# Top-k attention and two MLPs on one core: seven token chunks of 256 and 384 in place of six of 384

## The chip, the cores and the metric

The kernel runs on one core of a Trainium2 chip, in one launch. The metric is the device time of that core in microseconds (us), the median of several runs. Engines are named as the profile names them: PE (TensorE, with PEld for its weight loads), DVE (VectorE), ACT (ScalarE), POOL (GpSimd) and SP (SyncE, which issues every DMA here).

## The reference

```
# attention: batch 4, heads 8, sequence 576, head size 64, float32
scores = q @ k.T / 8
kth    = the 32nd largest score of each row
scores = where(scores >= kth, scores, -1e9)
attn   = exp(scores - max) / (sum + 1e-9)
a      = attn @ v                        # then [2304 tokens, 512]

# first MLP, w_in [512, 2048], w_out [2048, 512]
h = a @ w_in ;  y = (h - tanh(h)) @ w_out

# second MLP, same sizes
h = y @ w_in ;  out = where(h > 0, h, exp(min(h, 0)) - 1) @ w_out
```

## The kernel before

The 2304 tokens are cut into chunks (`CHUNKS`, L35). A chunk is a list of pieces (batch, first token, length). For each chunk and each of the four pairs of heads, attention is done in units: one unit per head where a piece has 256 tokens or more, and one unit for both heads together where it is shorter. A unit is made of tiles of 128 queries, and units are packed into groups of at most three tiles. In all there are 144 tiles, each of 128 queries by 576 keys.

The top-k of a tile is found on DVE: four times the eight largest values (`vm`, MAX8, L318) with three replacements of these by a very small number in between (`w`, MATCH_REPLACE8, L332). The 32nd value is then the threshold. The mask is applied in one of two ways: on DVE, which multiplies the exponentials that ACT has made by (score >= threshold) (L339), or on ACT, by a steep Prelu and an Exp (L334, L335). `MASK_ACT` says for how many tiles of a group in each chunk ACT does it.

The MLP of a chunk has 2 x 16 steps, one for each MLP and each block of 128 hidden columns. A step makes h from the chunk's tokens by 12 matmuls as wide as the chunk (`first`, L460: float32 is carried as a high and a low part, three products, four blocks of the contraction each), then the gate (`gate`: tanh or exp on ACT, `g` on DVE or by `GATE_GP` on POOL, the high part `gh` on ACT, the low part `gl` on POOL), and adds it to the output by three 512-wide matmuls for each 128 tokens (`second`, L496). The first two steps of the second MLP (`PARTED`) make h in two parts by columns.

The first time that weights are used they are prepared (`prepare`, L149 to L169): the raw 512 KB half is loaded, ACT, POOL, DVE (`wf`, L167) and ACT and POOL again turn it into a high and a low part, and the result is kept for the first chunk and written to DRAM. There are 64 such halves. Later chunks load them back (`wt`, L183), 1 MB for each step of each chunk, whatever the chunk's length.

The order is written out in ticks, four for a group: attention of chunk i+1 is laid beside the MLP steps of chunk i, with a group's loads, splits, scores, top-k and transposes at fixed distances. `starts` gives the tick of a chunk's first MLP step, and the MLP of the last chunk has nothing beside it. On top of this a scheduler orders each engine's instructions when the program is built, so the order that stands on an engine is seen in the built program and not in the source. Engines wait for each other by semaphores, and each works through its own list in order.

Of the kernel before, what the change touches and what calls it, by code (L numbers as in the profile page):

```python
# [8 lines left out]
F32 = mybir.dt.float32  # L9
F32R = mybir.dt.float32r  # L10
# [9 lines left out]
P = 128  # L20
# [12 lines left out]


CHUNKS = [  # L35
    [(0, 0, 384)],
    [(0, 384, 192), (1, 0, 192)],
    [(1, 192, 384)],
    [(2, 0, 384)],
    [(2, 384, 192), (3, 0, 192)],  # L40
    [(3, 192, 384)],
]
SIZES = [sum(n for _, _, n in c) for c in CHUNKS]
NMAX = max(SIZES)

MASK_ACT = [3, 1, 0, 0, 0, 0]

GATE_GP = [0, 0, 1, 1, 1, 2]

# [6 lines left out]

WI_BUFS = 5
WO_BUFS = 6  # L60
RAW_BUFS = 3
G_BUFS = 3
T_BUFS = 3
QR_BUFS = 2
KR_BUFS = 2
QS_BUFS = 2
KK_BUFS = 3
# [3 lines left out]
Y_BUFS = 3  # L71
E_BUFS = 6
W_BUFS = 3
G_BUFS = 3
T_BUFS = 3

FIRST_TICK = -8


SPARE = [5, 5, 5, 5, 5, 5]  # L80

QUICK = 6


NU = 384
# [1 line left out]
WHOLE = 1  # L87


DONE = [4, 8, 8, 8, 8, 8]  # L90


@with_exitstack
def tile_topk_attention_two_mlps(
# [11 lines left out]
    def pool(name, bufs, space=None):  # L106
        kw = {} if space is None else {"space": space}
        return ctx.enter_context(tc.tile_pool(name=name, bufs=bufs, **kw))

    const = pool("const", 1)  # L110
    sb = pool("sb", 2)
# [13 lines left out]
    def split(hi, lo, src):  # L125
        nc.scalar.activation(hi, src, copy)  # L126
        nc.gpsimd.tensor_sub(lo, src, f(hi))  # L127

    def bank(tag, name, bufs):
        return ps.tile([P, 512], F32, tag=tag, name=name, bufs=bufs)  # L130
# [15 lines left out]
    def prepare(m, ft, half):  # L146
# [3 lines left out]

        raw = sb.tile([P, 512], I64, tag="wr", name=f"wr{m}_{ft}_{half}", bufs=RAW_BUFS)
        nc.sync.dma_start(raw, (w1, w2)[m][ft][:, half * 512 : half * 512 + 512])
# [41 lines left out]
    for ci, size in enumerate(SIZES):  # L194
        for p in range(NPAIR):
# [22 lines left out]
            for us in cuts:  # L218
                g = Group()
# [11 lines left out]
    def hurried(u):  # L231

        return u.rush and u.last

    def quick(u):

        return u.ci < QUICK and u.p == NPAIR - 1 and u.g.at == chunk_end[u.ci] - 1

    def load_q(u):
        u.qraw = sb.tile([P, NU], F32, tag="qraw", name=f"qraw{u.id}", bufs=QR_BUFS)  # L240
        src = qT[u.b, 2 * u.p + u.heads[0] : 2 * u.p + u.heads[-1] + 1, :, u.q0 : u.q0 + u.n].rearrange("h d s -> d h s")
        nq = u.n * len(u.heads)
        for half in range(1 if u.whole else 2):
            nc.sync.dma_start(u.qraw[half * D : half * D + D, :nq].rearrange("d (h s) -> d h s", s=u.n), src)
# [54 lines left out]
    def topk_steps(g, r):  # L299
# [10 lines left out]

        by_act = 0 if g.rush and hurried(g.units[-1]) else min(k, MASK_ACT[g.units[0].ci])
        if r == 3 and by_act:
# [136 lines left out]
    def first(ci, m, ft):  # L449
        n = SIZES[ci]  # L450
        xh, xl = x_tiles[ci] if m == 0 else z_tiles[ci]
        h = bank("h", f"h{ci}_{m}_{ft}", 2)[:, :n]
        wv = weights.pop((ci, m, ft, 0)).rearrange("p a (k c) -> p a k c", c=P)
        jobs = [(wi, xs, kt) for wi, xs in ((0, xh), (1, xh), (0, xl)) for kt in range(4)]
        if m == 0 and ft == 0:
            jobs.sort(key=lambda x: x[2])
        late = (n // P - 1) * P
        for cs in (slice(0, late), slice(late, n)) if m == 1 and ft < PARTED and late else (slice(0, n),):
            for a, (wi, xs, kt) in enumerate(jobs):
                nc.tensor.matmul(h[:, cs], wv[:, wi, kt], xs[:, kt, cs], start=(a == 0), stop=(a == len(jobs) - 1))  # L460
        t = sb.tile([P, NMAX], F32, tag="t", name=f"t{ci}_{m}_{ft}", bufs=T_BUFS)[:, :n]
        if m == 0:
            nc.scalar.activation(t, h, AF.Tanh)
        else:
            nc.scalar.activation(t, h, AF.Relu, scale=-1.0)  # L465
            nc.scalar.activation(t, t, AF.Exp, scale=-1.0)  # L466
        parts[ci, m, ft] = h, t

    def gate(ci, m, ft):
        n = SIZES[ci]  # L470
        h, t = parts[ci, m, ft]
        g = sb.tile([P, NMAX], F32, tag="g", name=f"g{ci}_{m}_{ft}", bufs=T_BUFS)[:, :n]
        if m == 1:
            nc.vector.scalar_tensor_tensor(g, t, -1.0, h, op0=ALU.add, op1=ALU.max)  # L474
        elif ft % 4 < GATE_GP[ci]:
            nc.scalar.activation(g, h, copy)
            nc.gpsimd.tensor_sub(g, g, t)
        else:
            nc.vector.tensor_sub(g, h, t)  # L479
        gh = sb.tile([P, NMAX], F32R, tag="gh", name=f"gh{ci}_{m}_{ft}", bufs=G_BUFS)[:, :n]  # L480
        gl = sb.tile([P, NMAX], F32R, tag="gl", name=f"gl{ci}_{m}_{ft}", bufs=G_BUFS)[:, :n]
        split(gh, gl, g)
        parts[ci, m, ft] = gh, gl

# [49 lines left out]
    def step_parts(i):  # L534

        ci, m, ft = steps[i]
        nxt = steps[i + 1] if i + 1 < len(steps) else None
        turn = m == 0 and ft == NF - 1
        early = nxt is not None and not turn

        def a():
            if early:
                first(*nxt)

        def b():
            if early:
                gate(*nxt)

        def c():
            second(ci, m, ft)  # L550
            if turn:
                between(ci)
                first(*nxt)
                gate(*nxt)
            if m == 1 and ft == NF - 1:
                store(ci)
            load_next()

        return a, b, c
# [26 lines left out]

    n_ticks = 4 * len(groups) + DONE[-1]
    starts = [4 * e + d for e, d in zip(chunk_end, DONE)]
    at_tick = {}
    for ci in range(len(SIZES) - 1):  # L590
        ticks = starts[ci + 1] - starts[ci] - SPARE[ci]
        for j in range(ticks):
# [3 lines left out]
    for tick in range(FIRST_TICK, n_ticks):  # L596
# [8 lines left out]
        if tick == starts[0]:  # L605
            first(*steps[0])
            gate(*steps[0])
# [71 lines left out]
```

## Time and profile before

| | |
|---|---|
| time, median of 3 runs | 1267.47 us (1267.06 to 1269.64) |
| the profiled execution: its time, its span | 1266.36 us, 1264.3 us |
| PE busy | 1175.6 us, 93% |
| DVE busy | 992.0 us, 78% |
| ACT busy | 785.0 us, 62% |
| POOL busy | 603.2 us, 48% |
| moved by DMA | 286 MB, mean 226 GB/s |

The span is cut below at the first tanh of each chunk's MLP (171.8, 385.5, 565.0, 755.0, 940.9 and 1121.0 us). Called stages: stage A lasts to the first of them and has the attention of the first chunk, with a little of the second; stage 0 has the MLP of chunk 0 beside the attention of chunk 1 and the rest of the weight preparation; stages 1 to 4 have the MLP of that chunk beside the attention of the next; the last stage has the MLP of the last chunk alone. A matmul's duration in the trace is longer than the distance to the next one, since matmuls overlap; what a run of them costs is read from the starts.

### The profile page before, as it was taken

Reading aid. Unit: us, or ns where it says so; the run is one execution under the profiler, and the core shown is the slowest. Engines: PE = TensorE matmul, PEld = TensorE weight load, DVE = VectorE, ACT = ScalarE, POOL = GpSimd, SP = SyncE. Lnnn points to the kernel's source line nnn. Section 1 sums busy time; section 2 is a strip of 40 time slices with the busy share of each in tenths; the row PEclk is TensorE's granted clock in tenths of the full one; section 3 lists DMA queues with packets and bytes.
Section 4 is the critical chain, followed back from the end, with each engine's and each line's share of the span. In section 5 each row is a group of like instructions: output and inputs, shape, how many; then the busy total and the mean of one; then the engine's idle time right before and its main releaser. Section 6 shows DMA issues by size and latency. Waiting matters only on the chain.

```text
span 1264.3 us, 19733 instructions
## 1 busy us (share of the span) xinstructions
PE 1175.6 (93%) x6424; PEld 976.2 (77%) x6424; DVE 992.0 (78%) x1951; ACT 785.0 (62%) x1716; POOL 603.2 (48%) x629
## 2 busy tenths in 40 slices
PE   4477889989999999999999999999999999999998
PEld 2233467878779888888878888888888978889897
DVE  7999999999999999689999579898789988100111
ACT  5898868778876566465646566666555655433333
POOL 4786459779983433243433334434333422233222
PEclk9976699999999999999999999999999999999999
DMA  7886347988779665667657677756666546667672
GB/s 246 312 292 235 90 143 251 314 282 262 241 255 353 222 220 197 208 227 258 218 167 229 208 234 253 234 187 232 209 232 239 198 164 209 199 230 263 216 242 85
DMA packets 97446, 286.12 MB, mean 226 GB/s; under 512 B 12096, under 2 KB 27968, under 8 KB 97344
## 3 DMA queue, kind: packets, MB, share of 16 engines
q1 hardware_dynamic: 97344, 284.87, 67.4%
q8 instruction: 51, 0.84, 0.3%
q14 instruction: 51, 0.42, 0.1%
HBM read 246.55 MB, written 38.27 MB: 225 GB/s over the span
## 4 chain that ended last, share of the span: by engine, by line
PE 69%; DVE 14%; ACT 8%; DMA 5%; issue 3%; POOL 1%; SPq 0%; ACTq 0%; DVEq 0%; POOLq 0%
PE h L460 27%; PE acc L496 27%; PE av L378 6%; DVE vm L318 5%; DVE w L332 4%; DMA wr<-in_w_dram 4%; PE pt L360 4%; DVE wf L167 2%; PE ps L295 2%; PE ps L296 2%; DVE e L339 1%; ACT s L297 1%; ACT wr L162 1%; POOL wr L164 1%; ACT e L334 1%
## 5 line engine op out<-in xcount | busy, mean ns | idle before, releaser
L127 POOL TENSOR_TENSOR gl<-g,gh 128x384 fp32r<-128x384 f32 x192 | 206.1, 1075 | 315.0 <-ACT gh L126 292.1
L318 DVE MAX8 vm<-w 128x8 f32<-128x576 f32 x432 | 319.2, 751 | 3.9
L496 PE MATMUL acc<-wt,gh 128*128 128x512 f32 x1008 | 271.1, 398 | 0.7 <-ACT gh L126 0.7
L332 DVE MATCH_REPLACE8 w<-vm,w 128x576 f32<-128x576 f32 x288 | 213.3, 741 | 0.0
L496 PEld LDWEIGHTS acc<-wt,gh 128*128 128x128 f32 x1008 | 184.1, 188 | 33.9 <-ACT gh L126 1.6
L360 PE MATMUL pt<-ident,e 128*128 128x128 f32 (+1 forms) x720 | 119.7, 295 | 50.7 <-ACT e L335 35.8
L297 ACT ACTIVATE s<-ps 128x288 f32<-128x288 f32 (+1 forms) x320 | 124.5, 406 | 64.0 <-PE ps L296 56.5
L318 DVE MAX8 vm<-s 128x8 f32<-128x576 f32 x144 | 108.2, 752 | 62.0 <-ACT s L297 61.4
L360 PEld LDWEIGHTS pt<-ident,e 128*128 128x128 f32 (+1 forms) x720 | 90.1, 143 | 78.2 <-ACT e L335 42.0
L496 PE MATMUL acc<-wt,gl 128*128 128x512 f32 x504 | 149.9, 399 | 0.3 <-POOL gl L127 0.2
L460 PE MATMUL h<-zh,wt 128*128 128x384 f32 (+2 forms) x768 | 147.6, 325 | 2.6 <-ACT zh L515 1.8
L126 ACT ACTIVATE gh<-g 128x384 fp32r<-128x384 f32 x192 | 100.7, 526 | 74.7 <-DVE g L474 42.5
L460 PE MATMUL h<-xh,wt 128*128 128x384 f32 x672 | 144.7, 340 | 0.5 <-DVE g L479 0.2
L474 DVE SCALAR_TENSOR_TENSOR g<-t,h 128x384 f32<-128x384 f32 x96 | 52.3, 544 | 111.5 <-ACT t L466 111.3
L361 ACT ACTIVATE ph<-pt 128x384 f32<-128x384 f32 (+1 forms) x240 | 109.2, 491 | 40.9 <-PE pt L360 39.9
L460 PEld LDWEIGHTS h<-zh,wt 128*128 128x128 f32 x768 | 123.5, 188 | 13.5 <-ACT zh L515 3.2
L460 PEld LDWEIGHTS h<-xh,wt 128*128 128x128 f32 x672 | 117.7, 188 | 9.1 <-issue 1.2
L339 DVE SCALAR_TENSOR_TENSOR e<-s,vm,e 128x576 f32<-128x576 f32 x115 | 116.8, 1022 | 1.6 <-ACT e L322 0.5
L496 PEld LDWEIGHTS acc<-wt,gl 128*128 128x128 f32 x504 | 92.1, 188 | 20.2 <-issue 2.1
L164 POOL TENSOR_TENSOR wr<-wr,tiny 128x512 f16<-128x512 f32 x64 | 90.5, 1420 | 35.5 <-ACT wr L162 28.8
L332 DVE MATCH_REPLACE8 w<-vm,s 128x576 f32<-128x576 f32 x144 | 106.8, 741 | 0.0
L465 ACT ACTIVATE t<-h 128x384 f32<-128x384 f32 x96 | 46.9, 488 | 95.7 <-PE h L460 95.0
(80 smaller groups left out, 2018.2 us busy)
## 6 DMA issues: line engine op xcount, KB each, us to landing
wt<-w SPq DMA_DIRECT2D x336, 512.0 KB, 4.2
wr<-in_w_dram SPq DMA_DIRECT2D x64, 512.0 KB, 5.4
w<-wp SPq DMA_DIRECT2D x64, 512.0 KB, 4.2
kraw<-in_kT_dram SPq DMA_DIRECT2D x120, 144.0 KB, 3.9
vraw<-in_vL_dram SPq DMA_DIRECT2D x64, 160.0 KB, 3.1
qraw<-in_qT_dram SPq DMA_DIRECT2D x88, 96.0 KB, 3.3
out_dram<-o SPq DMA_DIRECT2D x16, 256.0 KB, 4.9
out_dram<-o SPq DMA_DIRECT2D x4, 128.0 KB, 4.7
```

The costliest lines, as they stand in the source:

```text
L126: nc.scalar.activation(hi, src, copy)
L127: nc.gpsimd.tensor_sub(lo, src, f(hi))
L164: nc.gpsimd.tensor_mul(top, scaled, tiny)
L297: nc.scalar.activation(s[lo:hi, cs], pt[lo:hi, :HS], copy)
L318: nc.vector.max(g.vm[:, j, min(r, 1)], u.s[t] if r == 0 else g.w[j])
L332: nc.vector.match_replace(g.w[j], v, u.s[t] if r == 0 else g.w[j], FILL)
L339: nc.vector.scalar_tensor_tensor(u.e[t], u.s[t], v[:, 7:8], u.e[t], op0=ALU.is_ge, op1=ALU.mult, accum_out=g.sum[:, j : j + 1])
L360: nc.tensor.transpose(pt[:kn, j * P : j * P + P], v.e[t][:, k0 : k0 + kn], ident)
L361: nc.scalar.activation(g.ph[:kn, blk, :nq], pt[:kn, :nq], copy)
L378: nc.tensor.matmul(pt[h * D : h * D + D, :n], v.vraw[h][:kn, blk], v.g.ph[:kn, blk, cs], start=(blk == 0), stop=(blk == NB - 1),)
L460: nc.tensor.matmul(h[:, cs], wv[:, wi, kt], xs[:, kt, cs], start=(a == 0), stop=(a == len(jobs) - 1))
L496: nc.tensor.matmul(acc[ci, m][t], gx[:, t * P : t * P + P], wt[:, wi], start=(ft == 0 and k == 0), stop=(ft == NF - 1 and k == 2),)
```

## The change

The tokens are cut into seven chunks of 256, 384, 384, 384, 384, 256 and 256. Four chunks are whole pieces of one batch, the fifth and sixth are made of two pieces, the last of one. `MASK_ACT` is 3 for the first two chunks: all tiles of the second chunk are masked on ACT, where one of three was before. `GATE_GP` and the other lists by chunk get a seventh entry; the sixth chunk keeps 2 and the seventh has 2. There are six buffers for raw weight halves instead of three, and three for q instead of two. The tiles t, g, gh and gl have the pool's two buffers each instead of three.

```
 CHUNKS = [
-    [(0, 0, 384)],
-    [(0, 384, 192), (1, 0, 192)],
-    [(1, 192, 384)],
+    [(0, 0, 256)],
+    [(1, 0, 384)],
     [(2, 0, 384)],
-    [(2, 384, 192), (3, 0, 192)],
-    [(3, 192, 384)],
+    [(3, 0, 384)],
+    [(1, 384, 192), (2, 384, 192)],
+    [(3, 384, 192), (0, 256, 64)],
+    [(0, 320, 256)],
 ]
-MASK_ACT = [3, 1, 0, 0, 0, 0]
+MASK_ACT = [3, 3, 0, 0, 0, 0, 0]
-GATE_GP = [0, 0, 1, 1, 1, 2]
+GATE_GP = [0, 0, 1, 1, 1, 2, 2]
-RAW_BUFS = 3
-G_BUFS = 3
-T_BUFS = 3
-QR_BUFS = 2
+RAW_BUFS = 6
+QR_BUFS = 3
-SPARE = [5, 5, 5, 5, 5, 5]
-QUICK = 6
+SPARE = [5, 5, 5, 5, 5, 5, 5]
+QUICK = 7
-DONE = [4, 8, 8, 8, 8, 8]
+DONE = [4, 8, 8, 8, 8, 8, 8]
...
-        t = sb.tile([P, NMAX], F32, tag="t", name=f"t{ci}_{m}_{ft}", bufs=T_BUFS)[:, :n]
+        t = sb.tile([P, NMAX], F32, tag="t", name=f"t{ci}_{m}_{ft}")[:, :n]
...
-        gl = sb.tile([P, NMAX], F32R, tag="gl", name=f"gl{ci}_{m}_{ft}", bufs=G_BUFS)[:, :n]
+        gl = sb.tile([P, NMAX], F32R, tag="gl", name=f"gl{ci}_{m}_{ft}")[:, :n]
```

Counted in the built programs, the work on each engine between the first MLP steps of the chunks is this (DVE: MAX8, MATCH_REPLACE8, masks, weight steps `wf`, gates; PE: matmuls of the MLP's first and second part; the stages of after carry their chunk's number).

| stage | before: MAX8, replace, mask, wf, gate | after | before: PE h, acc | after |
|---|---|---|---|---|
| A | 112, 83, 5, 29, 0 | 78, 58, 2, 29, 0 | 0, 0 | 0, 0 |
| 0 | 102, 78, 19, 35, 32 | 105, 80, 5, 35, 32 | 408, 276 | 408, 180 |
| 1 to 4 | 362, 271, 91, 0, 116 | 349, 261, 87, 0, 116 | 1632, 1155 | 1632, 1155 |
| 5 | 0, 0, 0, 0, 24 | 44, 33, 12, 0, 24 | 408, 297 | 408, 189 |
| 6 | | 0, 0, 0, 0, 24 | | 408, 204 |

On PE, where the first chunk's MLP begins, its name in the rows being h0_0_0 (chunk, MLP, block), this stood before; the transposes ahead of it belong to the third tile of the first chunk's last group:

```order
L360 MATMUL pt0_3_0_3_0_0_1_3_1315<-ident_66,e0_3_0_0_1_2_1151 128x128
L360 MATMUL pt0_3_0_3_0_0_1_4_1320<-ident_66,e0_3_0_0_1_2_1151 64x128
L460 MATMUL h0_0_0_1518<-xh0_499,wp0_0_0_1196 128x384 x2
L460 MATMUL h0_0_0_1518<-xl0_500,wp0_0_0_1196 128x384
L460 MATMUL h0_0_0_1518<-xh0_499,wp0_0_0_1196 128x384 x2
```

In the changed kernel, this stands there:

```order
L357 MATMUL pt0_3_0_3_0_0_0_4_989<-ident_66,e0_3_0_0_0_1_833 64x128
L292 MATMUL ps1_0_1_0_0_2_0_0_1021<-kk1_0_1_0_0_0_886,qs1_0_1_0_0_883 128x288
L293 MATMUL ps1_0_1_0_0_2_0_0_1021<-kk1_0_1_0_0_0_886,qs1_0_1_0_0_883 128x288
L457 MATMUL h0_0_0_1291<-xh0_427,wp0_0_0_1001 128x256 x2
L457 MATMUL h0_0_0_1291<-xl0_428,wp0_0_0_1001 128x256
L457 MATMUL h0_0_0_1291<-xh0_427,wp0_0_0_1001 128x256 x2
```

Eight tiles of attention fewer stand ahead of the first step, which is 256 columns wide; lines after the constants are three less than before.

On DVE, in the middle of stage 0, the end of a group of the second chunk (e1 is its second chunk's mask, g0 the gate of the first chunk's MLP) stood before as:

```order
L339 SCALAR_TENSOR_TENSOR e1_1_1_0_0_1_2290,sum1_1_1_1_1_0_0_2219<-s1_1_1_0_0_1_1989,vm1_1_1_1_1_0_0_2217,e1_1_1_0_0_1_2290 128x576
L318 MAX vm1_1_1_1_1_0_0_2217<-w31_1_1_1_1_0_0_2_2222 128x8
L479 TENSOR_TENSOR g0_0_11_2389<-h0_0_11_2361,t0_0_11_2374 128x384
L332 MATCH_REPLACE w31_2_1_2_0_384_0_0_2481<-vm1_2_1_2_0_384_0_2478,w31_2_1_2_0_384_0_0_2481 128x576
L339 SCALAR_TENSOR_TENSOR e1_1_1_0_0_2_2291,sum1_1_1_1_1_0_0_2219<-s1_1_1_0_0_2_2074,vm1_1_1_1_1_0_0_2217,e1_1_1_0_0_2_2291 128x576
```

The masks of the same pair of heads now stand on ACT:

```order
L331 ACTIVATE e1_1_1_0_0_2_1708<-s1_1_1_0_0_2_1497,nk1_1_1_1_1_0_0_1837 128x576
L294 ACTIVATE s1_1_1_0_1_2_1802<-ps1_1_1_0_1_2_0_1_1803 128x288
L294 ACTIVATE s1_1_1_0_1_2_1802<-ps1_1_1_0_1_2_1_1_1807 128x288
L257 ACTIVATE qs1_2_1_0_1_2095<-qraw1_2_1_0_1_1913 128x384
L123 ACTIVATE kk1_3_1_0_0_0_2349<-kraw1_3_1_0_0_0_2149 128x576
L460 ACTIVATE t0_0_11_2060<-h0_0_11_2047 128x256
L332 ACTIVATE e1_1_1_0_0_0_1706,sum1_1_1_1_1_0_0_1621<-e1_1_1_0_0_0_1706,b21_1_1_1_1_0_0_1838 128x576
L123 ACTIVATE gh0_0_10_2021<-g0_0_10_2019 128x256
```

DVE's mask instructions of that chunk left its list, and two ACT instructions for each stand between the copies of scores and gates.

## Rows read from the trace of the kernel before

**Rows 1.** The page's first lines: busy time, share, instructions.

```profile
span 1264.3 us, 19733 instructions
PE 1175.6 (93%) x6424; PEld 976.2 (77%) x6424; DVE 992.0 (78%) x1951; ACT 785.0 (62%) x1716; POOL 603.2 (48%) x629
```

**Rows 2.** Windows, one per stage: stretch, length, each engine's busy us (instructions), clock, DMA.

```profile
0.00:172.00 172.00, 113.01 (x369) 64.53 (x369) 157.45 (x317) 137.87 (x299) 105.55 (x122) 0.82 0.67 221
172.00:385.50 213.50, 195.38 (x1163) 164.26 (x1164) 210.04 (x375) 171.47 (x366) 184.58 (x171) 0.99 0.80 266
385.50:565.00 179.50, 178.05 (x1011) 153.47 (x1010) 159.82 (x330) 105.21 (x239) 65.01 (x72) 1.00 0.70 232
565.00:755.00 190.00, 188.57 (x1048) 159.44 (x1047) 161.28 (x327) 112.69 (x253) 72.08 (x79) 1.00 0.65 217
755.00:941.00 186.00, 184.32 (x1152) 161.57 (x1151) 160.84 (x321) 112.69 (x252) 78.54 (x82) 1.00 0.69 226
941.00:1121.00 180.00, 178.84 (x986) 150.38 (x985) 127.34 (x259) 95.50 (x215) 56.81 (x65) 1.00 0.59 200
1121.00:1264.00 143.00, 137.45 (x705) 122.52 (x703) 15.23 (x27) 49.60 (x100) 40.59 (x40) 1.00 0.61 211
```

**Rows 3.** Groups by line, DVE in stage A: count | busy, mean ns | idle before.

```profile
L318 DVE MAX8 vm<-w 128x8 f32<-128x576 f32 x81 | 59.6, 748 | 0.0
L332 DVE MATCH_REPLACE8 w<-vm,w 128x576 f32<-128x576 f32 x54 | 40.0, 742 | 0.0
...
L167 DVE SCALAR_TENSOR_TENSOR wf<-sc,wr 128x512 uint32<-128x512 uint32 x22 | 14.9, 678 | 2.5 <-POOL wr L164 2.4
L167 DVE SCALAR_TENSOR_TENSOR wf<-wr 128x512 uint32<-128x512 uint32 x7 | 6.1, 875 | 0.0
...
L339 DVE SCALAR_TENSOR_TENSOR e<-s,vm,e 128x576 f32<-128x576 f32 x4 | 4.0, 993 | 0.0
```

**Rows 4.** The same for DVE in stage 0.

```profile
L318 DVE MAX8 vm<-w 128x8 f32<-128x576 f32 x79 | 58.2, 746 | 0.4
L167 DVE SCALAR_TENSOR_TENSOR wf<-wr 128x512 uint32<-128x512 uint32 x35 | 42.7, 1221 | 0.3 <-POOL qs L261 0.3
L332 DVE MATCH_REPLACE8 w<-vm,w 128x576 f32<-128x576 f32 x52 | 38.3, 738 | 0.0
L339 DVE SCALAR_TENSOR_TENSOR e<-s,vm,e 128x576 f32<-128x576 f32 x21 | 26.7, 1277 | 0.0
...
L474 DVE SCALAR_TENSOR_TENSOR g<-t,h 128x384 f32<-128x384 f32 x16 | 8.6, 539 | 0.6 <-ACT t L466 0.5
```

**Rows 5.** The same for ACT in stage 0.

```profile
L335 ACT ACTIVATE e<-e,b 128x576 f32<-128x576 f32 x7 | 5.4, 777 | 0.0
L334 ACT ACTIVATE e<-s,nk 128x576 f32<-128x576 f32 x7 | 5.4, 773 | 0.2 <-POOL nk L324 0.2
```

**Rows 6.** Timeline of PE in the last stage: start, us, instructions merged.

```profile
1154.21 1.56 PE L496 MATMUL acc<-wt,gh 128*128 128x512 f32 x6
...
1156.31 1.55 PE L460 MATMUL h<-xh,wt 128*128 128x384 f32 x8
1157.69 0.86 PE L460 MATMUL h<-xl,wt 128*128 128x384 f32 x4
...
1192.00 0.63 PE L460 MATMUL h<-zl,wt 128*128 128x256 f32 x4
...
1192.47 1.00 PE L460 MATMUL h<-zh,wt 128*128 128x128 f32 x8
...
1193.31 1.13 PE L460 MATMUL h<-zl,wt 128*128 128x256 f32 x8
```

**Rows 7.** The chain that ended last: start, us, what; two attention products.

```profile
462.18 3.52 PE av L378 x20
...
788.97 3.70 PE av L378 x40
```

**Rows 8.** Windows: the busiest 30 us of the DMA engines; columns as in Rows 2.

```profile
380.00:410.00 30.00, 30.00 (x171) 27.65 (x170) 29.46 (x65) 19.89 (x46) 11.04 (x14) 1.00 1.03 354
```

More of the change, by code (lines that the diff above doesn't have):

```diff
@@ L73 @@
 W_BUFS = 3
-G_BUFS = 3
-T_BUFS = 3
 FIRST_TICK = -8
-SPARE = [5, 5, 5, 5, 5, 5]
-QUICK = 6
+SPARE = [5, 5, 5, 5, 5, 5, 5]
+QUICK = 7
 NU = 384
 WHOLE = 1
-DONE = [4, 8, 8, 8, 8, 8]
+DONE = [4, 8, 8, 8, 8, 8, 8]
 @with_exitstack
@@ L471, in gate @@
         h, t = parts[ci, m, ft]
-        g = sb.tile([P, NMAX], F32, tag="g", name=f"g{ci}_{m}_{ft}", bufs=T_BUFS)[:, :n]
+        g = sb.tile([P, NMAX], F32, tag="g", name=f"g{ci}_{m}_{ft}")[:, :n]
         if m == 1:
@@ L479, in gate @@
             nc.vector.tensor_sub(g, h, t)
-        gh = sb.tile([P, NMAX], F32R, tag="gh", name=f"gh{ci}_{m}_{ft}", bufs=G_BUFS)[:, :n]
-        gl = sb.tile([P, NMAX], F32R, tag="gl", name=f"gl{ci}_{m}_{ft}", bufs=G_BUFS)[:, :n]
+        gh = sb.tile([P, NMAX], F32R, tag="gh", name=f"gh{ci}_{m}_{ft}")[:, :n]
+        gl = sb.tile([P, NMAX], F32R, tag="gl", name=f"gl{ci}_{m}_{ft}")[:, :n]
         split(gh, gl, g)
```

## The prediction

> **What bounds the kernel now.** I read the page's first lines, then cut the span into stages by the first tanh of each chunk, then looked in each stage at which engine never rests, and at last at the cost of one instruction of that engine. PE is busy 93% of the span and DVE 78% [rows 1], but no engine is the bound throughout. The reader is to see in the stages [rows 2] that DVE binds the first two, with 157.45 of 172.0 us and 210.04 of 213.5, while PE works little in the first (113 us by its records, at a mean granted clock of 0.82) and in the second waits for what DVE hands over. From 385.5 us on PE is busy to within 1.2 to 1.7 us in each of the four middle stages and 5.5 us in the last, and it is the bound to the end. So a gain in DVE's work counts in stages A and 0, a change of PE's work counts after them, and anything else is hidden.
>
> **The change part by part.**
>
> *Stage A.* By the count of the built programs DVE does 34 MAX8, 25 replacements and 3 masks fewer before the first MLP step: 34 x 0.748 + 25 x 0.742 + 3 x 0.993 = 47.0 us [rows 3]. Records on DVE overlap a little: the groups of this stage add up to 175.7 us over all lines where 157.45 were busy [rows 2], so the time is 0.896 of that, 42.1 us. The 29 weight steps stay. DVE's idle time of 14.55 us stays too, except 2.5 us in which it waited for POOL's pass over a raw half [rows 3]; three more raw buffers let that pass run ahead. Stage A: 172.0 - 42.1 - 2.5 = 127.4 us.
>
> *Stage 0.* DVE gets 3 MAX8 and 2 replacements more, 3.7 us; 14 masks fewer at 1.277, 17.9 us; and 32 gates 256 wide. For these I take 0.41 us, between two thirds of the present 0.539 (0.36) and all of it, so 4.1 us less [rows 4]. Together -18.3 us, times 0.909 (210.04 busy where the groups add up to 231.0): -16.6 us, so 196.9 us. PE's work in this stage, by the prices worked out below, falls from 185.5 to 135.6 us, so PE is not the bound there. Nor is its clock: the granted clock, a mixture of 1.2 and 2.4 GHz, was 0.82 of the upper level over stage A and 0.99 over stage 0 [rows 2], and even 0.82 throughout would make 136 into 166 us, which fits into 197.
>
> *The masks on ACT.* Each costs two passes, 0.773 + 0.777 us [rows 5], and 14 exponentials of about the same 0.775 leave. With 17 more masks that is +26 and -11 us, and the narrower gates, wider whole pieces and fewer splits of k take about 15 us back, so ACT stays near its 171 us of work, now in 197 us: 0.87 busy against 0.80. I count nothing for it, because DVE at 0.98 still hides it; if ACT could be no busier than it is now, stage 0 would be 214 us, 17 us more.
>
> *A rule on the two engines that share a door.* In stage 0 the mask takes 1.277 us on DVE against 0.993 in stage A, and `wf` with both inputs in SBUF 1.221 against 0.678 for the form with one input in PSUM [rows 3, 4]; POOL is busy 0.86 of stage 0 and 0.61 of stage A [rows 2], while MAX8 with one input keeps 0.746 and 0.748. The Trainium skill, page "SBUF — State Buffer", section "Who interferes with whom", says that a VectorE instruction with two SBUF inputs and a GpSimd instruction that reads SBUF exclude each other, the later waiting for the whole of the earlier, and that one with a single SBUF input is not touched. The trace agrees. By that rule the masks that leave also free POOL, but the same 64 raw halves now pass through POOL in 324 us and not 385, so the 35 `wf` of stage 0 would stay near 1.2 us; the sum by it is the same within 2 us, but a large relief is spoken against.
>
> *Stages 1 to 4.* On PE I price by the distance of starts [rows 6]: nine 512-wide products in 2.10 us, 0.233 each; eight 384-wide in 1.38, 0.1725 each; four 256-wide in 0.47, 0.118 each; eight 128-wide in 0.84, 0.105 each. Scores, 288 wide, I take at 0.129, by width. An attention product of a head pair costs 3.52 us in ten 384-wide matmuls and 3.70 in twenty 192-wide [rows 7]; 256 wide I take 2.35 by width, and the 64-wide at the 192-wide price, 0.188 each, as the upper end. With the counts of the built program, the four stages of before are 709.6 us of PE and took 735.5 (a factor of 1.036, for switches between kinds of matmul and short waits); after they are 709.2 by the same prices, so they take 735.1. MLP work is unchanged there, whole pieces save a few scores and the 64-wide pieces give it back.
>
> *Stages 5 and 6 for the last stage.* Before: 138.0 us of PE (408 h products at 67.5, 297 acc at 69.3, transposes 1.3), and it took 143.3; the 5.3 us are the turn between the MLPs and the last store. After, stage 5 is 47.5 for h, 44.1 for acc, and 25.7 for the attention of the last chunk with its transposes: 117.3, times 1.036 is 121.6 us. Stage 6 is 96.0 and again 5.3: 101.3 us. A narrower product costs no more than its width, 0.118 against two thirds of 0.1725, 0.115: weight loads do not show at 256 columns. Together 222.9 us in place of 143.3, +79.6.
>
> *Buffers of t, g, gh and gl.* Two instead of three cost nothing in my sum: h has two banks before and after, so a gate two steps on must wait for the first in either kernel. Below, nothing is to be gained; above, as much as PE idles in the present last stage (5.5 us [rows 2]) once more in each of the last two, 11 us.
>
> *Loads.* A step loads 1 MB of weights whatever its width, so a seventh chunk adds 33.6 MB, and in stage 6 a step of 12 x 0.118 + 6 x 0.233 = 2.8 us wants 374 GB/s. The busiest 30 us gave 354 GB/s [rows 8]. Eleven weight tiles, 5.8 MB, are loaded ahead; stages 5 and 6 together want 2 x 33.6 MB and, for the last attention and the output, some 7 MB, so 74 MB in 223 us, 332 GB/s. I count nothing, since this lies under 354.
>
> *Sum.* Stage A -44.6, stage 0 -16.6, stages 1 to 4 -0.4, the end +79.6: +18.0 us. The span goes from 1264.3 to 1282.3; the profiled execution's time lies 2.1 us over its span and the median 1.1 us over that, so 1285.5. Since three of the prices are upper ends (64-wide products, all DVE idle time but 2.5 us, the full factor in stage 5), I take 3.5 us off: 1282 us. What the shorter end gains (42 us) and the shorter start (61 us) is more than taken back by the stage that is added between (122 us), because PE's work is the same for every token and DVE still has 24 tiles and 35 weight steps in the stage where the MLP has become short.
>
> **The rivals.**
>
> *DVE's stretch goes away (faster).* With six raw buffers, ACT and POOL prepare ahead, and DVE meets POOL less. If `wf` fell to the undisturbed 0.678 in stage 0, that is 35 x 0.543 x 0.909 = 17.3 us, and if of the 18.0 us that DVE idles in the two stages only the start's 7 us stayed, 8.5 more than I counted: 1282 - 26 = 1256 us. It decides from a `wf` below about 0.85 us together with half of that idle time. For it: 0.875 was seen in stage A [rows 3]. Against it: POOL becomes busier, not idler, in the shorter stages.
>
> *DMA binds the last two stages (slower still).* 74 MB at the 300 GB/s that a mixed stretch may give take 247 us and not 223: 1306 us. It decides below 332 GB/s. For it: the mean of stage 0, with many kinds of loads, was 266 GB/s at a share of 0.80, which is 333 at a full share [rows 2]. Against it: 354 in the busiest stretch, and buffers filled in stage 4, which moves only some 200.
>
> *ACT binds stage 0 (slower still).* As priced above: 1299 us.
>
> *The terms cancel.* If half of the first rival comes true, or the factor of 1.036 does not hold, 1267 us within 3.
>
> **How the numbers follow.** Forecast 0.50 (its own range 1272 to 1293), DMA 0.13, ACT 0.05, DVE's relief 0.22, cancelled 0.10. The range of 8 in 10 runs from 1256 to the DMA rival's 1306. 0.2% is 2.5 us, about what can be told from no change. Slower by more has the forecast, DMA and ACT, 0.68; the same 0.10; faster 0.22.
>
> **What would show it.** In the profile after: the first tanh near 127 us and that of the second chunk near 324; DVE busy over 0.95 of stage 0 and PE idle or waiting there, with records well under the 91% of now; `wf` from raw halves still near 1.2 us; the 256-wide products 0.118 us apart; stages 5 and 6 near 122 and 101 us. I am wrong if the second chunk's MLP begins before 306 us, or if the four stages after it take less than 715 us. More than 235 us for the last two stages, with DMA share near 1, would be the DMA rival.

## The result and the profile after

The changed kernel takes 1275.4 us, median of 4 runs (1274.3 to 1276.6), against 1268.4 us for the kernel before in 4 runs. The ratio is 1.0059 (95% interval 1.0041 to 1.0076): slower by some 7 us. The forecast was 1282 us and slower, so the way is right and the size is about half of what was forecast. The profiled execution has a span of 1273.5 us, 9.2 more than before. Two executions, one of the kernel before and the profiled one of e4 below, ran at a granted clock of 0.67 and 0.66 and took 1974.5 and 1671.3 us; they are left out of all times here.

Cut at the first tanh of each chunk, as in [rows 2], the windows of the changed kernel are these: stage A, stage 0, stages 1 to 4 in one row, stage 5 and stage 6. Columns as there.

```profile
0.00:128.70 128.70, 84.81 (x284) 46.44 (x284) 116.76 (x228) 112.20 (x257) 103.93 (x121) 0.99 0.88 305
128.70:317.40 188.70, 155.73 (x910) 127.34 (x911) 183.42 (x348) 161.92 (x381) 155.53 (x164) 0.92 0.81 281
317.40:1050.20 732.80, 725.36 (x4286) 625.27 (x4285) 586.54 (x1188) 429.25 (x973) 294.84 (x318) 1.00 0.71 227
1050.20:1174.60 124.40, 123.31 (x825) 105.57 (x824) 82.96 (x173) 72.12 (x196) 45.45 (x67) 1.00 0.81 279
1174.60:1273.50 98.90, 93.99 (x602) 83.88 (x600) 11.43 (x26) 37.42 (x96) 29.48 (x40) 0.99 0.82 310
```

In us, with DVE's busy time in brackets (the end is the last stage before, stages 5 and 6 after):

| stage | before | forecast | after |
|---|---|---|---|
| A | 172.0 (157.5 DVE) | 127.4 | 128.7 (116.8 DVE) |
| 0 | 213.5 (210.0 DVE) | 196.9 | 188.7 (183.4 DVE) |
| 1 to 4 | 735.5 | 735.1 | 732.8 |
| the end | 143.3 | 121.6 + 101.3 | 124.4 + 98.9 |

The start (stages A and 0) is 68 us shorter and the end 80 us longer. DVE is the busiest engine of the first two stages as before, PE of all later ones. In stage 0 the groups that answer to [rows 4] are these, in the same columns:

```profile
L315 DVE MAX8 vm<-w 128x8 f32<-128x576 f32 x81 | 59.5, 747 | 0.4
L329 DVE MATCH_REPLACE8 w<-vm,w 128x576 f32<-128x576 f32 x53 | 39.1, 738 | 0.0
L164 DVE SCALAR_TENSOR_TENSOR wf<-wr 128x512 uint32<-128x512 uint32 x35 | 38.1, 1090 | 1.3 <-POOL wp L124 1.1
...
L471 DVE SCALAR_TENSOR_TENSOR g<-t,h 128x256 f32<-128x256 f32 x16 | 6.3, 404 | 0.1
L336 DVE SCALAR_TENSOR_TENSOR e<-s,vm,e 128x576 f32<-128x576 f32 x4 | 4.2, 1061 | 0.0
```

The 256-wide gate came at 0.404 us (0.41 was taken), `wf` at 1.090 (near 1.2 was expected). DVE works 183.4 of the stage's 188.7 us and PE 155.7, which is what the prediction named as the sign that DVE binds. On PE, the timeline of stage 6 answers to [rows 6] (start, us, instructions):

```profile
1201.13 1.09 PE L493 MATMUL acc<-wt,gh 128*128 128x512 f32 x4
1202.06 0.63 PE L493 MATMUL acc<-wt,gl 128*128 128x512 f32 x2
1202.53 1.10 PE L457 MATMUL h<-xh,wt 128*128 128x256 f32 x8
1203.47 0.63 PE L457 MATMUL h<-xl,wt 128*128 128x256 f32 x4
1203.94 1.10 PE L493 MATMUL acc<-wt,gh 128*128 128x512 f32 x4
```

Twelve 256-wide products take 1.41 us (0.1175 each) and six 512-wide 1.40 (0.233), so a step is 2.81 us, as priced. Loads kept up with these steps, at 310 GB/s over the stage and a DMA share of 0.82.

### The profile page after: what moved, and what is told of

It is laid out like the page before. It is cut to its first block, busy times and chain, and to the rows that moved or that the text cites. A ratio compares the mean times of both kernels' runs of the same rounds, so it can differ in the third digit from the quotient of the medians.

```text
span 1273.5 us, 21441 instructions
## 1 busy us (share of the span) xinstructions
PE 1183.2 (93%) x6900; PEld 988.5 (78%) x6900; DVE 981.1 (77%) x1961; ACT 812.9 (64%) x1898; POOL 629.2 (49%) x709
## 4 chain that ended last, share of the span: by engine, by line
PE 74%; ACT 12%; DVE 7%; DMA 3%; issue 2%; POOL 1%; SPq 0%; ACTq 0%; POOLq 0%; DVEq 0%
PE h L457 30%; PE acc L493 29%; PE av L375 6%; PE pt L357 4%; DVE vm L315 3%; DMA wr<-in_w_dram 3%; DVE w L329 2%; PE ps L292 2%; PE ps L293 2%; ACT e L332 1%; ACT wr L159 1%; ACT wp L123 1%; ACT ph L358 1%; ACT s L294 1%; DVE wf L164 1%
## 5 line engine op out<-in xcount | busy, mean ns | idle before, releaser
L124 POOL TENSOR_TENSOR gl<-g,gh 128x384 fp32r<-128x384 f32 (+1 forms) x224 | 206.7, 925 | 347.9 <-ACT gh L123 309.2
L493 PE MATMUL acc<-wt,gh 128*128 128x512 f32 x1056 | 290.9, 400 | 1.2 <-ACT gh L123 1.2
L457 PE MATMUL h<-zh,wt 128*128 128x384 f32 (+2 forms) x912 | 162.4, 313 | 2.7 <-ACT zh L512 2.0
L123 ACT ACTIVATE gh<-g 128x384 fp32r<-128x384 f32 (+1 forms) x224 | 107.2, 482 | 77.9 <-DVE g L471 37.7
L457 PE MATMUL h<-xh,wt 128*128 128x384 f32 (+1 forms) x800 | 156.1, 319 | 0.5 <-DVE g L476 0.2
L358 ACT ACTIVATE ph<-pt 128x384 f32<-128x384 f32 (+2 forms) x280 | 116.5, 450 | 43.0 <-PE pt L357 41.9
L471 DVE SCALAR_TENSOR_TENSOR g<-t,h 128x384 f32<-128x384 f32 (+1 forms) x112 | 54.3, 487 | 97.6 <-ACT t L463 95.0
L462 ACT ACTIVATE t<-h 128x384 f32<-128x384 f32 (+1 forms) x112 | 49.6, 444 | 91.9 <-PE h L457 91.3
L124 POOL TENSOR_TENSOR kk<-kraw,kk 128x576 fp32r<-128x576 f32 x64 | 93.5, 1461 | 29.3 <-ACT kk L123 21.7
L375 PE MATMUL av<-ph,vraw 128*64 128x384 f32 (+7 forms) x720 | 103.5, 409 | 0.0
```

Source lines behind the costliest of these rows:

```text
L358: nc.scalar.activation(g.ph[:kn, blk, :nq], pt[:kn, :nq], copy)
L375: nc.tensor.matmul(pt[h * D : h * D + D, :n], v.vraw[h][:kn, blk], v.g.ph[:kn, blk, cs], start=(blk == 0), stop=(blk == NB - 1),)
L493: nc.tensor.matmul(acc[ci, m][t], gx[:, t * P : t * P + P], wt[:, wi], start=(ft == 0 and k == 0), stop=(ft == NF - 1 and k == 2),)
```

## The experiments

Each kernel was timed beside the kernel before, and ratios are to that; lengths come from its profiled execution, cut in the same way. That one execution lies up to 4 us from the median (e8's is 3.8 us under it, e2's 2.6 over), so a difference of a few us between two lengths is near the noise. The table holds what all of them say together, in us. "Start" is stages A and 0, with DVE's busy time in them; "rest" is all that comes after. "Masks" are the masks of the second chunk on ACT, "raw" is the number of buffers for raw weight halves, and "six whole" is the chunking of e3.

| kernel | median us | ratio (interval) | start: DVE busy of length | rest |
|---|---|---|---|---|
| before | 1266.5 to 1268.4 | 1 | 367.5 of 385.5 | 878.8 |
| changed | 1275.4 | 1.0059 (1.0041 to 1.0076) | 300.2 of 317.4 | 956.1 |
| e1, before + masks | 1273.9 | 1.0058 (1.0041 to 1.0075) | 346.0 of 393.4 | 879.1 |
| e2, changed - masks | 1280.7 | 1.0112 (1.0097 to 1.0126) | 309.2 of 321.9 | 959.6 |
| e3, six whole + masks | 1269.9 | 1.0025 (1.0017 to 1.0034) | 344.1 of 378.8 | 888.3 |
| e7, two chunks of 256 first | 1291.0 | 1.0190 (1.0176 to 1.0204) | 269.0 of 303.6 | 983.3 |
| e5, changed, 3 raw | 1292.0 | 1.0203 (1.0188 to 1.0219) | 310.3 of 333.5 | 956.5 |
| e8, before, 5 raw | 1275.0 | 1.0060 (1.0046 to 1.0074) | 367.0 of 391.8 | 877.6 |
| e9, before, 5 raw + masks | 1280.0 | 1.0103 (1.0089 to 1.0117) | 350.9 of 400.1 | 877.8 |
| e10, six whole, 5 raw | 1283.2 | 1.0129 (1.0114 to 1.0143) | 366.9 of 394.3 | 887.7 |
| e4, changed, third buffers, 5 raw | 1281.0 | 1.0106 (1.0087 to 1.0124) | - | - |
| e6, changed, less on POOL | 1278.4 | 1.0075 (1.0054 to 1.0095) | 295.3 of 322.9 | 955.3 |
| e11, split chunk second | 1278.0 | 1.0084 (1.0068 to 1.0099) | 302.3 of 330.3 | 945.7 |
| e12, before, DVE masks | 1274.1 | 1.0049 (1.0035 to 1.0063) | 369.5 of 393.1 | 879.1 |

**e1: the masks alone, on the kernel before.**

```
-MASK_ACT = [3, 1, 0, 0, 0, 0]
+MASK_ACT = [3, 3, 0, 0, 0, 0]
```

> The kernel before with the masks of the second chunk all on ACT, nothing else changed. Theory (DVE binds stage 0, and a mask that leaves it is worth its stretched time): 14 masks fewer in stage 0 at 1.277 us and 2 in stage A, times 0.91, are 18 us, so about 1250 us, stage 0 near 197 us. Rival (ACT, which takes about 16 us more in a stage where it would then be busy 0.95, binds instead): no gain, 1264 to 1270 us. Second rival (PE's 186 us of work times 1.036 ends the gain at 193 us): no less than 1247 us.

It was 7 us slower, and all of that in stage 0, whose row answers to the second of [rows 2]:

```profile
172.30:393.40 221.10, 199.50 (x1173) 172.80 (x1174) 188.69 (x349) 186.32 (x407) 177.63 (x174) 0.95 0.79 266
```

DVE has 21 us less to do and idles 32 us where it idled 3.5. Its largest waits are these (what waits, for what: total us, times, longest):

```profile
DVE vm L318 <- ACT s L297: 15.7, 7, 6.3
DVE wf L167 <- POOL wp L127: 4.0, 4, 1.4
DVE r L403 <- POOL r L400: 3.5, 1, 3.5
DVE g L474 <- ACT t L466: 3.0, 2, 2.5
```

The longest one is seen in ACT's timeline (start, us, instructions, idle before and its releaser):

```profile
248.93 0.41 ACT L297 ACTIVATE s<-ps 64x288 f32<-64x288 f32 x1
252.00 0.67 ACT L162 ACTIVATE wr<-wr 128x512 int32<-128x512 uint32 x1 [2.67 <-DMA wr<-in_w_dram]
252.69 0.40 ACT L297 ACTIVATE s<-ps 64x288 f32<-64x288 f32 x1
253.00 0.67 ACT L126 ACTIVATE kk<-kraw 128x576 fp32r<-128x576 f32 x1
254.15 0.68 ACT L166 ACTIVATE wr<-wr 128x512 f32<-128x512 f32 x1 [0.48 <-POOL wr L164]
254.85 0.41 ACT L297 ACTIVATE s<-ps 64x288 f32<-64x288 f32 x1
```

and in DVE's:

```profile
248.26 0.75 DVE L318 MAX8 vm<-w 128x8 f32<-128x576 f32 x1
255.29 0.76 DVE L318 MAX8 vm<-s 128x8 f32<-128x576 f32 x1 [6.28 <-ACT s L297]
```

ACT stands 2.67 us before a raw half that has not landed and 0.48 before POOL's pass over one; the copies of scores stand behind these and behind other work in its list, and DVE waits 6.28 us for the last of them. My theory was wrong here and its first rival nearer, though the time lies above that as well. DVE, no longer the fullest engine by far, waits on ACT for over half of its idle time, and on POOL for some 8 us. That the sum of ACT's work binds is not shown, since ACT is busy only 0.84 of the stage.

**e2: the changed kernel with the masks back on DVE.**

```
-MASK_ACT = [3, 3, 0, 0, 0, 0, 0]
+MASK_ACT = [3, 1, 0, 0, 0, 0, 0]
```

> The changed kernel with the masks of the second chunk as before, one of three on ACT. Theory: stage 0 gets the masks back on DVE, 14 to 16 at 1.1 to 1.28 us times 0.91, 14 to 18 us, and nothing else moves: about 1291 us. Rival (ACT binds stage 0 in the changed kernel, so the masks there are worth nothing): 1272 to 1278 us.

Slower than the changed kernel by 0.5% (ratios 1.0112 and 1.0059), some 6 us, between the two expectations. Its stage 0 and the groups of it on DVE:

```profile
131.30:321.90 190.60, 157.42 (x911) 126.76 (x910) 189.50 (x362) 149.87 (x345) 159.22 (x160) 0.91 0.78 268
```

```profile
L164 DVE SCALAR_TENSOR_TENSOR wf<-wr 128x512 uint32<-128x512 uint32 x35 | 35.9, 1027 | 1.1 <-POOL wp L124 1.1
L336 DVE SCALAR_TENSOR_TENSOR e<-s,vm,e 128x576 f32<-128x576 f32 x18 | 23.7, 1318 | 0.0
```

DVE is busy 189.5 of 190.6 us, so it is the bound here, and the stage is still 23 us shorter than before. With the masks on ACT the stage is only 1.9 us shorter than this, and the whole start 4.5. But the work in the stretch is not the same otherwise. In e2 the groups of top-k on `w` are these:

```profile
L315 DVE MAX8 vm<-w 128x8 f32<-128x576 f32 x75 | 54.0, 742 | 0.0
L329 DVE MATCH_REPLACE8 w<-vm,w 128x576 f32<-128x576 f32 x50 | 36.8, 737 | 0.0
```

They come to some 8 us less than in the changed kernel. So the 19.5 us of masks that leave DVE in the changed kernel are in part replaced there by top-k steps that in e2 stand in a neighbouring stage. DVE's busy time in stage 0 is lower by 6.1 us only, and its idle time higher by 4.2.

**e3: six whole chunks with the masks.**

```
-    [(0, 384, 192), (1, 0, 192)],
-    [(1, 192, 384)],
+    [(1, 0, 384)],
     [(2, 0, 384)],
-    [(2, 384, 192), (3, 0, 192)],
-    [(3, 192, 384)],
+    [(3, 0, 384)],
+    [(0, 384, 192), (1, 384, 192)],
+    [(2, 384, 192), (3, 384, 192)],
...
-MASK_ACT = [3, 1, 0, 0, 0, 0]
+MASK_ACT = [3, 3, 0, 0, 0, 0]
```

> Six chunks of 384 as before, but the first four are whole pieces of one batch each and the last two are made of two pieces each, and the masks of the second chunk are all on ACT; buffers as before. Theory: the last stage is not added, so the gain of the masks stays, and the whole pieces take six splits of k off ACT and POOL and 6 us off PE in stage 0: 1246 to 1250 us. Rival (the gain of the chunking lies in the short first chunk): 1262 us or more.

1269.9 us, the rival's side. Against the kernel before, the start fell by 6.7 us and stages 1 to 4 rose by 9:

```profile
173.40:378.80 205.40, 187.72 (x1007) 157.18 (x1008) 185.92 (x345) 175.87 (x388) 169.11 (x167) 0.97 0.78 263
378.80:1123.10 744.30, 738.70 (x4356) 636.55 (x4355) 605.28 (x1233) 438.06 (x975) 288.60 (x305) 1.00 0.69 220
```

PE is 8.9 us longer busy in those stages, with some 160 matmuls more. So the further matmuls of a chunk made of two pieces, behind DVE while it was the second chunk, are paid in a stage where PE binds. What the whole pieces do for the start apart from the masks is not shown by this run, which has both edits.

**e7: the second chunk at 256 as well.**

```
     [(0, 0, 256)],
-    [(1, 0, 384)],
+    [(1, 0, 256)],
     [(2, 0, 384)],
     [(3, 0, 384)],
-    [(1, 384, 192), (2, 384, 192)],
-    [(3, 384, 192), (0, 256, 64)],
-    [(0, 320, 256)],
+    [(0, 256, 192), (1, 256, 192)],
+    [(2, 384, 192), (3, 384, 192)],
+    [(0, 448, 128), (1, 448, 128)],
```

> The changed kernel with the second chunk at 256 tokens too (256, 256, four of 384, 256; the last three made of two pieces). Theory (DVE binds stages A, 0 and 1, PE all later ones): stage 0 falls by 31 us to about 158, stage 1 (MLP of 256 beside attention of 384) is about 150 us by DVE, later stages 734 and 98: about 1269 us. Rival (the weight preparation, by POOL busy 152 us and DMA at 330 GB/s, binds stage 0 at 168 us or more): 1279 us or more.

The rival, and by more: DVE has 31 us less to do in stage 0 and the stage is only 12 us shorter than in the changed kernel.

```profile
127.40:303.60 176.20, 145.91 (x856) 117.61 (x857) 152.83 (x283) 147.66 (x360) 153.95 (x162) 0.92 0.83 287
```

```profile
DVE wf L164 <- POOL wp L124: 10.2, 6, 4.2
DVE g L471 <- ACT t L463: 8.4, 2, 4.4
```

The second view gives DVE's largest waits there, as in e1: for POOL's part of the weight preparation and for ACT's exponentials in the second MLP. POOL is now as busy as DVE. Stage 1 was 143 us (150 expected) and the later ones 740 and 100 (734 and 98).

**e5: the changed kernel with three raw buffers.**

```
-RAW_BUFS = 6
+RAW_BUFS = 3
```

> The changed kernel with three raw weight buffers instead of six. New theory (masks on ACT pay only where ACT's list is not held up by raw loads, which the third to sixth buffer bring forward): stage 0 grows by some 15 to 20 us as DVE comes to wait for copies of scores, 1290 to 1297 us. Rival (raw buffers hide nothing; the masks did better in the changed kernel because its gates and splits of k leave ACT less to do): 1274 to 1280 us.

1292.0 us, within what the new theory said. All of the loss against the changed kernel is in the start:

```profile
0.00:135.00 135.00, 80.13 (x284) 45.26 (x284) 117.39 (x228) 109.67 (x251) 100.51 (x118) 0.81 0.84 279
135.00:333.50 198.50, 160.37 (x923) 128.53 (x924) 192.95 (x365) 170.73 (x400) 162.71 (x168) 0.92 0.75 260
```

But the reason given is borne out only in part: DVE idles 6 us more over the start, and is busy 10 us more. Another order stands on it, which puts more of the top-k ahead of the second chunk's MLP (85 MAX8 on `w` in this stretch and 81 in the changed kernel's), and `wf` takes 1.126 us.

**e8, e9 and e10: five raw buffers on the kernel before, without the masks (e8) and with them (e9), and without them on the six chunks of e3 (e10).**

```
-RAW_BUFS = 3
+RAW_BUFS = 5
```

> The kernel before with five raw weight buffers instead of three, nothing else changed. New theory: DVE is busy 0.98 of stage 0 there, so the waits of ACT for raw loads are hidden: 1262 to 1267 us. Rival (ACT's 17 us of waiting for raw loads set the pace): 1250 to 1258 us.

> The kernel before with five raw buffers and the second chunk's masks all on ACT. New theory: with the raw loads ahead the masks pay here too, at least in part: 1252 to 1262 us. Rival (ACT has too much in stage 0 of this kernel, whatever the buffers): 1270 us or more, as in the run with the masks alone.

> Six chunks of 384, the first four whole pieces, five raw buffers, masks as before on DVE for two of three tiles in the second chunk. New theory: stage 0 stays bound by DVE but loses POOL's six splits of k, which DVE's two-input operations meet, and PE's 6 us: 1255 to 1264 us. Rival (the split pieces cost the same wherever they stand): 1264 to 1269 us.

The lines above are e8's edit; e9 adds e1's to it, and e10 the chunks of e3. They took 1275.0, 1280.0 and 1283.2 us: only the rival of e9 came true, and e8 and e10 are slower than anything expected of them. The start of e8:

```profile
0.00:181.20 181.20, 114.15 (x371) 63.51 (x371) 164.50 (x325) 139.94 (x302) 107.29 (x125) 0.82 0.65 216
181.20:391.80 210.60, 194.84 (x1183) 165.21 (x1184) 202.51 (x371) 172.37 (x372) 181.72 (x169) 1.00 0.82 281
```

DVE's work is the same 367 us as before, and it idles 6.8 us more. So six raw buffers instead of three are worth 16 us in the changed kernel, and five instead of three cost 7 in the one before; the masks likewise pay some 6 or cost 7. The theory that the one edit needs the other falls with e9: in the kernel before, they do not help together either. In the built programs each of these edits also reorders DVE's list of some 1400 instructions: to turn the order of the kernel before into that of e1, some 18% of the instructions that both have must change places, and 24% for e8, though none by more than 17 places. So a run shows an edit together with the order that the scheduler makes of it. The two could not be told apart by these runs, and why an order is better by 7 us stays open.

**e12: the kernel before with all masks of the second chunk on DVE.**

```
-MASK_ACT = [3, 1, 0, 0, 0, 0]
+MASK_ACT = [3, 0, 0, 0, 0, 0]
```

> The kernel before with the masks of the second chunk all on DVE. Theory (DVE is busy 0.98 of stage 0, so what is added to it is paid in full, though what is taken off and given to ACT brought nothing): eight masks at 1.28 us times 0.91 are 9 us, 1274 to 1278 us. Rival (ACT sets the pace of stage 0, and every mask that it loses is a gain): 1255 to 1264 us.

As expected in total, 1274.1 us, but not by DVE's work, which rose by 2 us only: it idles 5.6 us more. So from the kernel before, a step in either direction costs some 7 us.

**e6: less on POOL.** The pass that scales the raw halves for the last term of the weights' rounding is left out.

```
-        nc.gpsimd.tensor_mul(top, scaled, tiny)
```

> The changed kernel with POOL's pass over the raw halves left out (the last term of the rounding of the weights is not formed, 64 instructions of about 1.4 us on POOL). Theory (DVE's two-input steps are stretched by what POOL does, and POOL stands in the chain of the preparation): the weight step in stage 0 falls from 1.09 us to 1.0 or less, and stages A and 0 together get 5 to 10 us shorter, 1265 to 1270 us. Rival (raw loads set the pace of the preparation): 1273 us or more, with the weight step still shorter.

Stage 0 and its weight step:

```profile
131.60:322.90 191.30, 159.27 (x921) 127.29 (x922) 179.55 (x355) 164.34 (x384) 112.95 (x135) 0.92 0.82 283
```

```profile
L163 DVE SCALAR_TENSOR_TENSOR wf<-wr 128x512 uint32<-128x512 uint32 x35 | 30.7, 876 | 3.5 <-POOL wp L124 3.5
```

With POOL busy 0.59 of the stage instead of 0.82, `wf` fell from 1.090 to 0.876 us, so in this pair of runs the stretch does come from POOL's work. That is the rule of the Trainium skill, page "SBUF — State Buffer", section "Who interferes with whom", on a VectorE instruction with two SBUF inputs, and this run agrees with it. But the stage did not get shorter (the rival): DVE worked 4 us less and idled 6 us more. The prediction's rival in which DVE's stretch goes away and the kernel is faster has its mechanism here and not its gain.

**e11: the chunk of two 192-token pieces in second place, the three whole ones behind it.**

```
     [(0, 0, 256)],
+    [(1, 384, 192), (2, 384, 192)],
     [(1, 0, 384)],
     [(2, 0, 384)],
     [(3, 0, 384)],
-    [(1, 384, 192), (2, 384, 192)],
```

> The changed kernel with the chunk of two 192-token pieces moved from fifth to second place, the three whole ones behind it. Theory (PE has slack in stage 0 alone, and the further score, product and transpose matmuls of the two pieces, 8 us, stand behind DVE there): stages 1 to 6 lose 8 us, stage 0 keeps its 189 us, so about 1267 us. Rival (stage 0 has no slack: eight more splits of k on ACT and POOL hold DVE up): stage 0 is 8 us or more longer, 1275 us or more.

Both halves happened:

```profile
133.40:330.30 196.90, 165.68 (x1081) 136.13 (x1081) 181.85 (x337) 171.25 (x397) 164.26 (x171) 0.95 0.85 292
330.30:1052.90 722.60, 715.44 (x4105) 613.00 (x4105) 589.35 (x1195) 417.73 (x950) 280.23 (x309) 1.00 0.70 223
```

The middle stages lose 10 us, near the 8 counted on PE, and the start grows by 13, of which 8 are in stage 0, with less work on DVE there than in the changed kernel. DVE idles 15 us in that stage and not 5, most of it for POOL:

```profile
DVE wf L164 <- POOL wp L124: 6.0, 7, 1.5
DVE r L400 <- POOL r L397: 4.2, 2, 3.2
```

POOL and ACT are each 9 us longer busy there. That the eight further splits of k are the cause fits this, but the order changed with them, and no run parts the two.

**e4: three buffers again for t, g, gh and gl, and five raw buffers to make room.**

```
-RAW_BUFS = 6
+RAW_BUFS = 5
...
-        t = sb.tile([P, NMAX], F32, tag="t", name=f"t{ci}_{m}_{ft}")[:, :n]
+        t = sb.tile([P, NMAX], F32, tag="t", name=f"t{ci}_{m}_{ft}", bufs=3)[:, :n]
...
```

> The changed kernel with three buffers each for t, g, gh and gl as before, and five raw buffers instead of six to make room. Theory (the third buffers are worth nothing, h's two banks hold the gates back anyway): 1273 to 1278 us. Rival (each of the last stages loses by them): 1264 to 1270 us.

1281.0 us, above both expectations and slower than the changed kernel. No trace tells where the time goes. The third buffers bring nothing that outweighs one raw buffer; what each does alone stays open.

No kernel tried here beats the one before. The nearest is e3, at 1.0025.

## Why the prediction was right

**What binds.** DVE in stages A and 0, PE after them: this holds, and the part on PE holds closely. The rest after stage 0 is 877.6 to 879.1 us in the five kernels with the chunks of before and 955.3 to 959.6 in the four traced with the chunks of the change. The four middle stages were 732.8 us for a forecast of 735.1, the two last ones 223.3 for 222.9. The end was the term that decided the sign, +80.0 us measured and +79.6 forecast, against 68 us that the start gained.

**The size.** The terms of the sum came to +18.0 us and the spans differ by +9.2: stage A lies 1.3 us above its term, stage 0 8.2 below, stages 1 to 4 2.3 below and the end 0.4 above. The 3.5 us that were taken off the sum were for prices in stage A and in the later stages, where the sum was right within 1 us in all; nearly all of the difference is in stage 0.

**Stage A.** 128.7 us for 127.4. Here taking work off DVE shortened the stage almost one for one: 40.7 us less work, 43.3 us less time.

**Stage 0.** This is the mis-sized term: -16.6 us in the prediction, -24.8 measured, and by another way. I gave nearly all of it to the 14 masks, at 16.3 us. Undone, they are worth 1.9 us there, 4.5 over the start and 5.3 by the medians of the whole (e2), since other work and idle time of DVE took most of their place. What I put at about nothing, the shorter chunk with its buffers, is worth 22.9 us: in e2, `wf` takes 1.027 us and not 1.221, 6.8 us for 35; the gates come to 4.2 us less; and the stretch holds fewer of the top-k steps, some 5 us by the groups of MAX8 and replacements. The two errors cancelled in part, and that the stage came out within 8 us of its forecast is in part luck. The mechanism, that DVE is the bound, was right for the sign of the term and wrong for the price of a single edit: e1's waits show that a mask taken off DVE need not be a gain when ACT, which gets it, must also deliver what DVE works on next.

**ACT hides the masks.** Wrong in the kernel before, where DVE's idle time in stage 0 went from 3.5 to 32 us with them (e1); in the changed kernel ACT is busy 0.86 of the stage (0.87 forecast), DVE idles 5.3 us, and it held.

**DVE's relief, the rival at 0.22.** Neither of its conditions came: `wf` was 1.090 us, not below 0.85, and DVE idles 17.2 us over stages A and 0 where it idled 18.0.

**Clock.** As forecast it does not bind stage 0: it was granted 0.92 there, a mixture of the 1.2 and 2.4 GHz levels, and PE worked 156 of 189 us. In stage A it was 0.99, and in e5, with nearly the same work, 0.81, where DVE idled 18 us and not 12. The clock alone does not explain that: e2, with the changed kernel's raw buffers, ran its stage A at 0.82, and DVE idled 11.6 us:

```profile
0.00:131.30 131.30, 83.28 (x290) 46.46 (x290) 119.67 (x233) 114.70 (x262) 105.22 (x124) 0.82 0.86 299
```

Over whole runs of the changed kernel it decides nothing: a mean of 0.986 went with 1275.3 us, 0.970 with 1276.6 and 0.972 with 1274.3.

**Buffers, loads.** The third buffers of the gate: no gain seen in e4. DMA in the last stages, the rival at 0.13: not seen, 279 and 310 GB/s with PE busy 0.99 and 0.95. That is 65 MB in 223 us, 293 GB/s; the prediction had counted 74 MB and 332 GB/s, so less had to be moved than it said.

**Where the gain of the shorter chunks went.** A shorter first chunk brings 43 us and a shorter last one 44, and stage 0 25, and a stage of 124 us is added, since the MLP and attention of the tokens moved out of them must still pass through PE. The time that PE idles while DVE binds did not fall at all: by its records, whose ends are modelled, PE rested 77.1 us of stages A and 0 before (385.5 less 113.0 and 195.4, [rows 2]) and rests 76.9 after (317.4 less 84.8 and 155.7). Of the 9.2 us, 7.6 are PE's busy time by the same records, 1175.6 us before [rows 1] and 1183.2 after. Why it grew is not shown; the matmuls are some 480 more and on the whole narrower.

## What to carry to other kernels

Price each stage by the engine that binds it, and when work is moved between chunks, follow it to the stage where it is paid: here 80 us at the end against 68 at the start gave the sign. Where several in-order engines are near full and feed each other, the price of a single edit is not its own work: waits and work moved in from a neighbouring stage can take its place. Take the price from a run in which that edit is undone in the kernel at hand; masks on ACT and more raw buffers were worth some 6 and 16 us in one kernel and cost 7 each in the other.

## What was not expected of the hardware

The stretch of a two-input DVE instruction comes with POOL's work, but POOL's busy share does not give its size. With POOL busy 0.59 of stage 0 (e6) `wf` took 0.876 us, and 0.678 with one input in PSUM [rows 3]. With POOL busy 0.80 to 0.87 it took from 1.012 (e3) to 1.221 us [rows 4], in no order of the share. In e9 and e7, whose windows had POOL at 0.80 and 0.87:

```profile
179.80:400.10 220.30, 201.67 (x1180) 175.91 (x1180) 186.43 (x338) 182.20 (x400) 175.77 (x169) 0.93 0.79 264
L167 DVE SCALAR_TENSOR_TENSOR wf<-wr 128x512 uint32<-128x512 uint32 x35 | 39.5, 1131 | 4.1 <-POOL wp L127 4.0
L164 DVE SCALAR_TENSOR_TENSOR wf<-wr 128x512 uint32<-128x512 uint32 x35 | 37.6, 1074 | 10.6 <-POOL wp L124 10.2 <-DMA vraw<-in_vL_dram 0.3
```

Relieving it was worth nothing in time. As was priced, PE's own loads of its weights do not show at 256 columns in stage 6: 0.1175 us for each product, near two thirds of the 0.1725 at 384.
